# A third PSUM bank for a mixture-of-experts layer, and attention's turning and values in one bank

## The chip, the core and the metric

The kernel runs on one core of a Trainium2 chip. It uses the core's five engines: TensorE (matrix products), VectorE, ScalarE, GpSimd and SyncE, which issues nearly all the transfers. Each engine takes its own instructions in order and waits on semaphores for the others. The metric is the time on the device of one execution, in microseconds (us). Before the change it was 956.05 us, the median of three runs from 955.3 to 958.82.

## What is computed

Three layers follow each other: attention with a mask by blocks of 64 positions (8 batches, 8 heads, 576 positions, 64 dimensions a head), a dense layer with an exponential unit between two weight matrices (4608 tokens, 512 to 2048 and back to 512), and a soft mixture of 8 experts with 4 slots each.

```python
scores = scale * np.matmul(q, k.transpose(0, 1, 3, 2))
scores = np.where(block_i >= block_j, scores, -1e9)
attn = softmax(scores)                               # over the last axis
x = np.matmul(attn, v)                               # -> 4608 tokens x 512

h = x @ w_in                                         # 512 -> 2048, "first layer"
g = np.where(h > 0.0, h, np.exp(np.minimum(h, 0.0)) - 1.0)
x = g @ w_out                                        # 2048 -> 512

logits = x @ phi                                     # 512 -> 32 slots
d = softmax(logits, axis=0); slot_input = d.T @ x    # over all tokens
slot_out[e] = np.maximum(slot_input[e] @ w1[e], 0.0) @ w2[e]
c = softmax(logits, axis=1)
out = c @ slot_out
```

## The kernel before, in words

**Work units.** Attention is done for 32 pairs of heads (`n`, four pairs for each batch). The dense layer and the routing are done for 36 tiles of 128 tokens (`i`), and the first layer of a tile in four ranges of 512 columns (`r`). `w_out` is not applied to tokens: the product `w_out @ phi` is made at the start (`WP`), the logits come from the 2048 values `g` directly, and the slots gather `g`. The experts and the output follow in `tail`.

**Order.** Every step is entered into `Plan` with its engines, an estimated duration, the keys of what it reads and writes, and a due time (`key`). `Plan.order` simulates the engines with these estimates and each time gives a free engine the ready step with the smallest due time; the resulting order is the instruction order of the program. A tile has 22 units of due time, its ranges 5.5 each; a pair's steps start at a due time of its own and are spread over some 24 units. The planner knows of conflicts only what the keys say. What an instruction must really wait for is put in afterwards, from the memory that it touches.

**PSUM.** There are eight banks of 512 columns. `H0` and `H0 + 512` (keys `("h", 0)`, `("h", 1)`) take the first layer's ranges in turn, `GTB` the slot products, `POST` (key `"post"`) the routing, `SB0` and `SB0 + 512` the scores, `PTB` (key `"ptb"`) the turned weights of attention and the first 128 columns of the values, and `PVB` (key `"pvb"`) the other 448 columns of the values.

**A range** (`tile_range`, lines 800 to 828): 12 products into its bank (lines 808 to 810, in four steps of three), then ScalarE's exponent from the bank into a buffer `E` (line 813), VectorE's minimum and minus one on that buffer (line 815), and VectorE's maximum of the buffer and the bank into the range's output slot `g` (line 818). Only after the maximum is the bank free. For tiles 0 to 29 a stream transpose on VectorE (line 826) and two transfers (`tile_turn`) turn the output for the logits. There are 12 output slots for tiles 5 to 29, otherwise 8; four of the 12 lie in another area, which the trace calls att.

**Routing** (`tile_routing`, `tile_dispatch`): logits into `POST` columns 0 to 127 (line 853) and, in the same step, the slot products of the tile before into `GTB` (line 919); then copies, sums and maxima in `POST` up to column 415 (lines 876 to 904) in turn on VectorE, TensorE and ScalarE.

**A pair from the ninth on** (`n` at least 8): scores in four fills of the `SB0` banks (lines 564 to 577), row maxima (line 587), exponents (line 590), division on GpSimd (line 607), then some blocks turned by TensorE through `PTB` in three groups (`pair_swap`, line 700, through the transpose helper at line 360) and copied out on ScalarE or VectorE, and the others turned by stream transposes and transfers through DRAM (line 689, `swapped`). `swapped_values` then makes the products with the values (line 739): 18 of them, each in two passes, two running side by side on the two halves of the columns. The copy helper is at lines 336 and 338.

Of the kernel before, what the change touches and what calls it, by code (L numbers as in the profile page):

```python
# [18 lines left out]
P = 128  # L19
# [8 lines left out]
NEV, NQ = 16, 1  # L28
TLAG, LATE, NTP, JOINED = 2.5, 30, 8, 5
EARLY = 16.0  # L30
CHANGE, STAY, JOIN = 0.13, 0.0, 0.0
TICK, DUTY, FILL, FN = 3.4, 0.5, 0.055, 128
SCALE = 0.125
# [205 lines left out]
def attention_moe_kernel(ctx: ExitStack, tc, q, k, v, w_in, w_out, phi, w1, w2, consts, out):  # L239
# [13 lines left out]
    C = base.take(NTILE * NS)  # L253
# [57 lines left out]
    def f(o, n, p0=0, p1=P):  # L311
        return view(as_f32, o, n, p0, p1)
# [21 lines left out]
    def copy(e, o, i):  # L334
        if e == "ACT":
            nc.scalar.copy(o, i)  # L336
        else:
            nc.vector.tensor_copy(o, i)
# [10 lines left out]
    def evict(n, w):  # L349

        return (CP2, cpdur(w)) if n >= NEV else ("ACT", cpdur(w)[0])
# [317 lines left out]
    def swap_keys(sl):  # L669
        return [("px", sl, x) for x in UNITS] + [("px", sl, m) for m in range(len(MOVES))] + [("py", sl, g) for g in range(3)]  # L670
# [6 lines left out]
    def pair_swap(n, half, key):  # L677

        sl = n % 2
        px, py = PX + 4 * XW * sl, PY + 2 * YW * sl  # L680
        if n == NTP and half == 0:
            handover(swap_keys(0) + swap_keys(1), [x for y in range(NPT) for x in pt_keys[y]])
        for x in HALVES[half]:
            if x == "b" or x[0] == 0:
                continue
            cs = min(x[0] + 1, 3)
            at, _, step = spots(x[0], x[1], 0)
            o = f(px, 4 * XW).rearrange("p (m b j) -> p b m j", m=4, j=32)[:, at:at + step * (cs - 1) + 1:step]
            add("DVE", 0.12 + P * cs / 960, lambda e, x=x, o=o, cs=cs: nc.vector.transpose(  # L689
                out=o, in_=f(pat(x, n), P * cs).rearrange("p (c m i) -> p c m i", c=cs, m=4)),  # L690
                r=[pkey(x, n)], w=[("px", sl, x)], key=key)
        both = f(py, 2 * YW).rearrange("p (h w) -> p h w", h=2)
        groups = ([("b", c) for c in range(4)], [((3, 0), 3), ((3, 1), 3), ("b", 4)]) if half == 0 else ([((0, 0), 0), ((0, 1), 0)],)
        for gi, blocks in enumerate(groups):
            g = gi + 2 * half
            tb, tk = (PTB, "ptb")

            def tr(e, blocks=blocks, tb=tb):
                for j, (x, c) in enumerate(blocks):
                    transpose(pb(tb + P * j, P), f(pat(x, n) + P * c, P))  # L700
            add("PE", 0.02 + 0.108 * len(blocks), tr, r=[pkey(x, n) for x in {b[0]: 0 for b in blocks}] + ["con"], w=[tk], key=key, load=0.0)

            def evac(e, g=g, tb=tb):
                if g == 0:
                    src = pb(tb, 512).rearrange("p (c h x) -> p h c x", c=4, h=2)
                    copy(e, both[:, :, P:P + 192].rearrange("p h (c x) -> p h c x", c=3), src[:, :, 0:3])
                    copy(e, both[:, :, 448:512], src[:, :, 3])
                elif g == 1:
                    copy(e, both[:, :, 320:448], pb(tb, 256).rearrange("p (h x) -> p h x", h=2))
                    copy(e, both[:, :, 512:576], pb(tb + 256, P).rearrange("p (h x) -> p h x", h=2))  # L710
                else:
                    copy(e, both[:, :, 0:P], pb(tb, 256).rearrange("p (h x) -> p h x", h=2))
            add(*evict(n, (560, 430, 256)[g]), evac, r=[tk], w=[("py", sl, g)], key=key)
        if half == 0:
            return
        via = swapped[sl]
        load(via, f(px, 4 * XW), 4 * P * 4 * XW, r=[("px", sl, x) for x in UNITS], w=[("pvia", sl)], key=key, lag=TLAG)
        for j, (m, a0, a1) in enumerate(MOVES):
            load(f(px + XW * a0, XW * (a1 - a0), 32 * m, 32 * m + 32).rearrange("i (a y) -> i a y", y=XW),
                 via.rearrange("(a i) (m y) -> m i a y", a=4, m=4)[m][:, a0:a1], 200 * (a1 - a0) * XW,  # L720
                 r=[("pvia", sl)], w=[("px", sl, j)], key=key, lag=TLAG)

    def swapped_values(n, key):
        b, p = divmod(n, 4)
        sl = n % 2
        vs = V + 640 * (n % NV)
        px = f(PX + 4 * XW * sl, 4 * XW).rearrange("p (a b j) -> p b a j", a=4, j=32)
        both = f(PY + 2 * YW * sl, 2 * YW).rearrange("p (h w) -> p h w", h=2)
        ring = XR + RING * p + S * (b % 2)

        def far(h, c):
            u = max(c, 1)
            at, step, _ = spots(u, h, c)
            return px[:, at:at + step * (3 - u) + 1:step]

        def pv(e):
            def go(o, w, c, rhs, start, stop):
                for h in range(2):
                    mm(pb(o, w, 64 * h, 64 * h + 64), lhsT=f(vs + 320 * h + D * c, D), rhs=rhs(h), start=start, stop=stop)  # L739
            go(PTB, P, 0, lambda h: both[:, h, 0:P], True, True)  # L740
            for c in range(3):
                w = P * (4 - max(c, 1))
                go(PVB + 384 - w, w, c, lambda h: far(h, c), c == 0, False)
                go(PVB + 384, 64, c, lambda h: both[:, h, P + 64 * c:P + 64 * c + 64], False, False)
            go(PVB + 256, 192, 3, lambda h: both[:, h, 320:512], False, False)
            go(PVB + 384, 64, 4, lambda h: both[:, h, 512:576], False, True)
        add("PE", 3.0, pv, r=[("v", n % NV, j) for j in range(3)] + swap_keys(sl), w=["ptb", "pvb"], key=key, load=0.25, mode="C")
        add(*evict(n, P), lambda e: copy(e, f(ring, P), pb(PTB, P)), r=["ptb"], w=[("xr", p, b % 2, 0)], key=key)
        add(*evict(n, 448), lambda e: copy(e, f(ring + P, 448), pb(PVB, 448)), r=["pvb"], w=[("xr", p, b % 2, 1)], key=key)

    def pair_values(n, key):
        if n >= NTP:
# [45 lines left out]
            r=xr_keys + [("xh", s)], w=[("xl", s)], key=key)  # L798

    def tile_range(i, r, hb, gs, ts, kr):  # L800
        s = i % 2
        xh, xl = XH + 512 * s, XL + 512 * s
        g, gk = gs
        bank, ee = H0 + 512 * hb, E + 512 * hb
        for kk in range(4):
            def hm(e, kk=kk):
                hi, lo = fr(W[r] + 512 * kk, 512), fr(W[r] + PIECE + 512 * kk, 512)
                mm(pb(bank, 512), lhsT=fr(xh + P * kk, P), rhs=hi, start=(kk == 0), stop=False)  # L808
                mm(pb(bank, 512), lhsT=fr(xh + P * kk, P), rhs=lo, start=False, stop=False)  # L809
                mm(pb(bank, 512), lhsT=fr(xl + P * kk, P), rhs=hi, start=False, stop=(kk == 3))  # L810
            marks["hm"] = len(plan.ops)
            add("PE", 0.7, hm, r=[("xh", s), ("xl", s), ("wh", r, kk), ("wl", r, kk)], w=[("h", hb)], key=kr)
        add("ACT", 0.48, lambda e: nc.scalar.activation(f(ee, 512), pb(bank, 512), AF.Exp),  # L813
            r=[("h", hb)], w=[("e", hb)], key=kr)
        add("DVE", 0.335, lambda e: nc.vector.tensor_scalar(  # L815
            out=f(ee, 512), in0=f(ee, 512), scalar1=1.0, scalar2=-1.0, op0=ALU.min, op1=ALU.add),
            w=[("e", hb)], key=kr)
        add("DVE", 0.6, lambda e: nc.vector.tensor_tensor(  # L818
            out=f(g, 512), in0=f(ee, 512), in1=pb(bank, 512), op=ALU.max),
            r=[("e", hb), ("h", hb)], w=[gk], key=kr)  # L820

        if ts is None:

            hf = r // 2
            tt = f(TG[s] + 1024 * hf, 1024).rearrange("p (b c j) -> p c b j", b=4, j=32)[:, 4 * (r % 2):4 * (r % 2) + 4]
            add("DVE", 0.7, lambda e: nc.vector.transpose(out=tt, in_=f(g, 512).rearrange("p (c b i) -> p c b i", c=4, i=32)),  # L826
                r=[gk], w=[("tg", s, hf, "ab"[r % 2])], key=kr)
            return

        def gtr(e):  # L830
            for j in range(4):
                transpose(pb(GTB + P * j, P), f(g + P * j, P))
        add("PE", 0.44, gtr, r=[gk, "con"], w=["gtb"], key=kr, load=0.0)
        add(CP2, cpdur(512), lambda e: copy(e, f(ts[0], 512), pb(GTB, 512)), r=["gtb"], w=ts[1], key=kr)
# [133 lines left out]
    def tail(key):  # L968
# [61 lines left out]

        B = [512 * j for j in range(8)]
        bk = ["h0t", "h1t", "gtbt", "postt", "s0t", "s1t", "ptbt", "pvbt"]
        for nm, old in zip(bk, (("h", 0), ("h", 1), "gtb", "post", ("sb", 0), ("sb", 1), "ptb", "pvb")):
            handover([nm], [old])

# [199 lines left out]
```

## Time and profile before

| | |
|---|---|
| median of 3 runs | 956.05 us (955.3 to 958.82) |
| profiled execution | 955.77 us |
| span in its profile | 954.0 us |
| TensorE busy | 908.7 us, 95% |
| VectorE busy | 675.9 us, 71% |
| ScalarE busy | 439.4 us, 46% |
| GpSimd busy | 272.6 us, 29% |
| first product of tile 6, of tile 31 | 251.9, 782.7 us |
| mean granted clock of TensorE | 0.99 of full |

How to read it: the span runs from the first to the last instruction of one execution, and the runs' own time is a little longer. Busy time counts an engine's instructions at work, overlaps once; products are pipelined, so two that overlap count as one stretch, and a busy TensorE is not one at its peak. "Idle before" is the time in which nothing of an engine ran, put down to the instruction of another engine that came last before the next one started. In the rows PE is TensorE, DVE VectorE, ACT ScalarE, and L808 is line 808.

### The profile page before, as it was taken

Reading aid. Unit: us, or ns where it says so; the run is one execution under the profiler, and the core shown is the slowest. Engines: PE = TensorE matmul, PEld = TensorE weight load, DVE = VectorE, ACT = ScalarE, POOL = GpSimd, SP = SyncE. Lnnn points to the kernel's source line nnn. Section 1 sums busy time; section 2 is a strip of 40 time slices with the busy share of each in tenths; the row PEclk is TensorE's granted clock in tenths of the full one; section 3 lists DMA queues with packets and bytes.
Section 4 is the critical chain, followed back from the end, with each engine's and each line's share of the span. In section 5 each row is a group of like instructions: output and inputs, shape, how many; then the busy total and the mean of one; then the engine's idle time right before and its main releaser. Section 6 shows DMA issues by size and latency. Waiting matters only on the chain.

```text
span 954.0 us, 19403 instructions
## 1 busy us (share of the span) xinstructions
PE 908.7 (95%) x6708; PEld 623.3 (65%) x6708; DVE 675.9 (71%) x1718; ACT 439.4 (46%) x1285; POOL 272.6 (29%) x428
## 2 busy tenths in 40 slices
PE   8889999999999999999999999999999999999992
PEld 6556777666666766676766666766776776766350
DVE  5887795668787887777888878887887844333160
ACT  5775655445445535444445445444444333322143
POOL 2863442133342332222323432332332210000000
PEclk9999999999999999999999999999999999999996
DMA  9846755647777785767677777667756498068969
GB/s 235 243 130 171 220 184 159 146 115 207 202 203 218 197 209 184 212 181 211 194 203 206 199 208 201 202 188 203 206 163 217 144 305 340 3 216 298 377 223 342
DMA packets 253217, 197.08 MB, mean 207 GB/s; under 512 B 183232, under 2 KB 206400, under 8 KB 250048
## 3 DMA queue, kind: packets, MB, share of 16 engines
q1 hardware_dynamic: 251920, 195.55, 69.1%
q8 instruction: 54, 0.88, 0.4%
q10 hardware_dynamic: 1200, 0.30, 0.1%
q14 instruction: 43, 0.35, 0.1%
HBM read 125.52 MB, written 70.25 MB: 205 GB/s over the span
## 4 chain that ended last, share of the span: by engine, by line
PE 74%; DVE 8%; DMA 7%; SPq 4%; ACT 2%; issue 2%; POOL 1%; ACTq 0%; DVEq 0%; POOLq 0%
PE ps L808 13%; PE ps L810 11%; PE ps L809 11%; PE ps L360 8%; PE ps L576 7%; PE ps L739 7%; SPq L355 4%; PE ps L919 3%; PE ps L568 2%; PE ps L853 2%; DMA att<-swapped 2%; DMA swapped<-att 2%; PE ps L767 2%; DVE base L587 2%; PE ps L460 1%
## 5 line engine op out<-in xcount | busy, mean ns | idle before, releaser
L808 PE MATMUL ps<-w,xhl 128*128 128x512 f32 x576 | 249.8, 434 | 7.8 <-DVE g L818 5.5
L607 POOL TENSOR_SCALAR att<-att,base 128x128 f32<-128x128 f32 (+4 forms) x288 | 181.0, 647 | 222.2 <-DVE base L603 151.0
L810 PE MATMUL ps<-w,xhl 128*128 128x512 f32 x576 | 226.8, 394 | 0.0
L809 PE MATMUL ps<-w,xhl 128*128 128x512 f32 x576 | 225.7, 392 | 0.0
L590 ACT ACTIVATE att<-ps,base 128x128 f32<-128x128 f32 (+4 forms) x288 | 157.4, 552 | 122.9 <-DVE base L587 121.0
L587 DVE TENSOR_REDUCE base<-ps 128x1 f32<-128x128 f32 (+4 forms) x288 | 135.7, 503 | 21.3 <-PE ps L572 12.2
L808 PEld LDWEIGHTS ps<-w,xhl 128*128 128x128 f32 x576 | 108.8, 189 | 52.0 <-issue 19.1
L813 ACT ACTIVATE xe<-ps 128x512 f32<-128x512 f32 x144 | 86.0, 600 | 115.0 <-PE ps L810 113.7
L810 PEld LDWEIGHTS ps<-w,xhl 128*128 128x128 f32 x576 | 108.1, 188 | 24.9
L336 ACT COPY att<-ps 128x128 f32<-128x128 f32 (+3 forms) x192 | 75.7, 434 | 95.8 <-PE ps L360 90.6
L809 PEld LDWEIGHTS ps<-w,xhl 128*128 128x128 f32 x576 | 108.9, 189 | 14.8
L815 DVE TENSOR_SCALAR xe<-xe 128x512 f32<-128x512 f32 x144 | 68.1, 473 | 67.0 <-ACT xe L813 65.6
L576 PE MATMUL ps<-att 64*128 64x128 f32 (+3 forms) x512 | 96.1, 468 | 1.0 <-ACT att L590 1.0
L360 PE MATMUL ps<-base,att 128*128 128x128 f32 (+1 forms) x496 | 83.2, 282 | 9.7 <-POOL att L607 8.5
L360 PEld LDWEIGHTS ps<-base,att 128*128 128x128 f32 (+1 forms) x496 | 58.0, 143 | 44.5 <-POOL att L607 17.6
L795 POOL TENSOR_TENSOR xhl<-xe,xhl 128x512 fp32r<-128x512 f32 x36 | 46.3, 1291 | 133.1 <-ACT xhl L793 127.0
L818 DVE TENSOR_TENSOR g<-xe,ps 128x512 f32<-128x512 f32 x108 | 73.3, 680 | 2.4
L689 DVE STREAM_TRANSPOSE att<-att 128x384 f32<-128x384 f32 x144 | 70.4, 507 | 5.3 <-POOL att L607 4.2
L739 PE MATMUL ps<-att 128*64 128x64 f32 (+4 forms) x864 | 71.9, 318 | 1.2 <-DMA att<-swapped 0.7
L576 PEld LDWEIGHTS ps<-att 64*128 64x128 f32 x512 | 42.0, 185 | 40.6 <-issue 14.1
L739 PEld LDWEIGHTS ps<-att 128*64 128x64 f32 x864 | 46.8, 137 | 32.3 <-issue 23.6
L826 DVE STREAM_TRANSPOSE g<-g 128x512 f32<-128x512 f32 x84 | 58.0, 695 | 1.7 <-DMA turned<-g 0.2
(134 smaller groups left out, 1115.1 us busy)
## 6 DMA issues: line engine op xcount, KB each, us to landing
turned<-g SPq DMA_DIRECT2D x60, 512.0 KB, 3.1
swapped<-att SPq DMA_DIRECT2D x24, 1024.0 KB, 4.6
g<-turned SPq DMA_DIRECT2D x120, 96.0 KB, 2.6
att<-in_moe_w_dram SPq DMA_DIRECT2D x11, 1024.0 KB, 11.8
att<-swapped SPq DMA_DIRECT2D x48, 192.0 KB, 3.9
att<-in_v_dram SPq DMA_DIRECT2D x64, 128.0 KB, 3.2
g<-in_moe_w_in_dram SPq DMA_DIRECT2D x16, 512.0 KB, 5.3
w_late<-in_moe_w_dram SPq DMA_DIRECT2D x8, 1024.0 KB, 6.9
```

The lines of the kernel that those rows point to most:

```text
L336: nc.scalar.copy(o, i)
L360: mm(o, lhsT=i, rhs=f(IDN + base, n, base, base + n), start=True, stop=True, is_transpose=True)
L576: mm(pb(at((u, h)), P * (u + 1)), lhsT=f(qt + P * u, P, 64 * h, 64 * h + 64), rhs=f(kt, P * (u + 1), 64 * h, 64 * h + 64), start=True, sto ...
L587: add("DVE", 0.08 + wide(x) / 960, lambda e, x=x, c=c: nc.vector.tensor_reduce(out=f(c, 1), in_=pb(at(x), wide(x)), axis=AX.X, op=ALU.max, ...
L590: add("ACT", 0.50 + wide(x) / 1300, lambda e, x=x, c=c: nc.scalar.activation(f(pat(x, n), wide(x)), pb(at(x), wide(x)), AF.Exp, bias=f(c, ...
L607: add("POOL", (0.28 + wide(x) / 1050) * (1.3 if n < 8 else 1.0), lambda e, x=x, p=p: nc.gpsimd.tensor_scalar(out=f(p, wide(x)), in0=f(p, w ...
L739: mm(pb(o, w, 64 * h, 64 * h + 64), lhsT=f(vs + 320 * h + D * c, D), rhs=rhs(h), start=start, stop=stop)
L808: mm(pb(bank, 512), lhsT=fr(xh + P * kk, P), rhs=hi, start=(kk == 0), stop=False)
L809: mm(pb(bank, 512), lhsT=fr(xh + P * kk, P), rhs=lo, start=False, stop=False)
L810: mm(pb(bank, 512), lhsT=fr(xl + P * kk, P), rhs=hi, start=False, stop=(kk == 3))
L813: add("ACT", 0.48, lambda e: nc.scalar.activation(f(ee, 512), pb(bank, 512), AF.Exp), r=[("h", hb)], w=[("e", hb)], key=kr)
L818: add("DVE", 0.6, lambda e: nc.vector.tensor_tensor(out=f(g, 512), in0=f(ee, 512), in1=pb(bank, 512), op=ALU.max), r=[("e", hb), ("h", hb) ...
```

## The change

From tile 6 to tile 33 the ranges of the first layer take three banks in turn, the third being `PTB`. In these tiles the exponent is written to the output slot and minimum and maximum work there in place; the buffer `E` isn't used. For pairs from the ninth on, the turned groups and the first 512 columns of the values go through `PVB`, and the last 64 columns of the values into the last 64 columns of `POST` under a new key `"pvx"`. The products of the values are split anew (20 instead of 18, the same columns in all), and the two copies are of 512 and 64 columns instead of 128 and 448.

```diff
+THREE = (6, 34)
 ...
@@ pair_swap
-            tb, tk = (PTB, "ptb")
+            tb, tk = (PVB, "pvb")
@@ swapped_values
-            go(PTB, P, 0, lambda h: both[:, h, 0:P], True, True)
+            go(PVB, P, 0, lambda h: both[:, h, 0:P], True, True)
             for c in range(3):
                 w = P * (4 - max(c, 1))
-                go(PVB + 384 - w, w, c, lambda h: far(h, c), c == 0, False)
-                go(PVB + 384, 64, c, lambda h: both[:, h, P + 64 * c:P + 64 * c + 64], False, False)
-            go(PVB + 256, 192, 3, lambda h: both[:, h, 320:512], False, False)
-            go(PVB + 384, 64, 4, lambda h: both[:, h, 512:576], False, True)
-        add("PE", 3.0, pv, r=[("v", n % NV, j) for j in range(3)] + swap_keys(sl), w=["ptb", "pvb"], key=key, load=0.25, mode="C")
-        add(*evict(n, P), lambda e: copy(e, f(ring, P), pb(PTB, P)), r=["ptb"], w=[("xr", p, b % 2, 0)], key=key)
-        add(*evict(n, 448), lambda e: copy(e, f(ring + P, 448), pb(PVB, 448)), r=["pvb"], w=[("xr", p, b % 2, 1)], key=key)
+                go(PVB + 512 - w, w, c, lambda h: far(h, c), c == 0, False)
+            go(PVB + 384, P, 3, lambda h: both[:, h, 320:448], False, True)
+            for c in range(5):
+                x = P + 64 * c if c < 3 else 64 * c + 256
+                go(POST + 448, 64, c, lambda h: both[:, h, x:x + 64], c == 0, c == 4)
+        add("PE", 3.0, pv, r=[("v", n % NV, j) for j in range(3)] + swap_keys(sl), w=["pvb", "pvx"], key=key, load=0.25, mode="C")
+        add(*evict(n, 512), lambda e: copy(e, f(ring, 512), pb(PVB, 512)), r=["pvb"], w=[("xr", p, b % 2, 0)], key=key)
+        add(*evict(n, 64), lambda e: copy(e, f(ring + 512, 64), pb(POST + 448, 64)), r=["pvx"], w=[("xr", p, b % 2, 1)], key=key)
@@ tile_range
+        three = THREE[0] <= i < THREE[1]
+        if three:
+            hb = (4 * i + r) % 3
+        if (i, r) == (THREE[0], 0):
+            handover([("h", 2)], ["ptb"])
-        bank, ee = H0 + 512 * hb, E + 512 * hb
+        bank, ee, ek = ((H0, H0 + 512, PTB)[hb], g, gk) if three else (H0 + 512 * hb, E + 512 * hb, ("e", hb))
 ...
         add("ACT", 0.48, lambda e: nc.scalar.activation(f(ee, 512), pb(bank, 512), AF.Exp),
-            r=[("h", hb)], w=[("e", hb)], key=kr)
+            r=[("h", hb)], w=[ek], key=kr)
 ...
-            w=[("e", hb)], key=kr)
+            w=[ek], key=kr)
 ...
-            r=[("e", hb), ("h", hb)], w=[gk], key=kr)
+            r=[ek, ("h", hb)], w=[gk], key=kr)
@@ tail
+        handover(["ptb"], [("h", 2)])
+        handover(["post"], ["pvx"])
```

## Rows read from the trace of the kernel before

**Rows 1.** The page, part 1: busy us (share of span) and instructions of each engine.

```profile
PE 908.7 (95%) x6708; PEld 623.3 (65%) x6708; DVE 675.9 (71%) x1718; ACT 439.4 (46%) x1285; POOL 272.6 (29%) x428
```

**Rows 2.** Busy us by stretch: PE, PEld, DVE, ACT, POOL (instructions), clock, DMA share, GB/s.

```profile
251.90:782.70 530.80, 522.58 (x3772) 364.46 (x3770) 426.23 (x1124) 241.57 (x765) 164.87 (x281) 1.00 0.71 201
...
866.50:954.00 87.50, 66.18 (x574) 32.79 (x574) 26.17 (x52) 26.50 (x55) 0.00 (x0) 0.91 0.86 313
```

**Rows 3.** Waits of TensorE from 250 to 782.7: us in total, times, longest.

```profile
PE ps L808 <- DVE g L818: 3.5, 5, 0.9
PE ps L808 <- DVE att L818: 2.2, 3, 1.0
PE ps L360 <- DVE base L924: 0.9, 1, 0.9
...
PE ps L360 <- ACT base L889: 0.2, 1, 0.2
```

**Rows 4.** Waits of TensorE from 120 to 250.

```profile
PE ps L808 <- DVE g L818: 2.0, 1, 2.0
```

**Rows 5.** Instructions in order, 343.5 to 348: start, us, engine, line, [idle before <-releaser].

```profile
345.42 0.40 PE L810 MATMUL ps<-w,xhl 128*128 128x512 f32 x1
...
346.00 0.69 DVE L818 TENSOR_TENSOR g<-xe,ps 128x512 f32<-128x512 f32 x1
...
346.75 0.50 PE L808 MATMUL ps<-w,xhl 128*128 128x512 f32 x1 [0.93 <-DVE g L818]
...
346.99 0.60 ACT L813 ACTIVATE xe<-ps 128x512 f32<-128x512 f32 x1
347.08 0.40 PE L809 MATMUL ps<-w,xhl 128*128 128x512 f32 x1
347.31 0.39 PE L810 MATMUL ps<-w,xhl 128*128 128x512 f32 x1
```

**Rows 6.** Instructions in order, 334.5 to 344: values, logits and slot products, an exponent.

```profile
335.69 2.95 PE L739 MATMUL ps<-att 128*64 128x128 f32 x36
...
338.57 1.08 PE L853 MATMUL ps<-g,base 128*32 128x128 f32 x32
...
339.46 1.04 PE L919 MATMUL ps<-g,base 128*32 128x512 f32 x8
...
342.52 0.60 ACT L813 ACTIVATE xe<-ps 128x512 f32<-128x512 f32 x1 [2.88 <-PE ps L810]
```

**Rows 7.** Instructions in order, 473.5 to 479: values, their second copy, turning.

```profile
473.92 2.95 PE L739 MATMUL ps<-att 128*64 128x128 f32 x36
...
477.05 0.58 DVE L338 COPY xe<-ps 128x448 f32<-128x448 f32 x1
...
477.44 0.66 PE L360 MATMUL ps<-base,att 128*128 128x128 f32 x4
```

**Rows 8.** Line 336, ScalarE's copies of the values: ns min/median/max, first and last start, forms.

```profile
L336 ACT COPY xe<-ps x51: 202/267/598, 42.7 to 776.0; 128x128 f32<-128x128 f32 x23, 128x448 f32<-128x448 f32 x12, 128x64 f32<-128x64 f32 x8, 128x512 f32<-128x512 f32 x8
```

**Rows 9.** Instructions in order, 659 to 664.5: routing steps during the values.

```profile
660.04 2.95 PE L739 MATMUL ps<-att 128*64 128x128 f32 x36
...
660.68 0.25 DVE L885 TENSOR_REDUCE base<-ps 128x1 f32<-128x128 f32 x1
...
661.41 0.36 ACT L889 ACTIVATE base<-ps,base 128x128 f32<-128x128 f32 x1
...
662.92 0.33 PE L360 MATMUL ps<-base 128*128 128x128 f32 x1
```

**Rows 10.** TensorE in order, 764 to 786: last pair's values, tile 31.

```profile
776.34 2.73 PE L739 MATMUL ps<-att 128*64 128x384 f32 x32 [0.49 <-DMA att<-swapped]
...
781.81 0.66 PE L360 MATMUL ps<-base,g 128*128 128x128 f32 x4 [0.87 <-DVE base L924]
...
782.67 0.48 PE L808 MATMUL ps<-w,xhl 128*128 128x512 f32 x1
```

## The prediction

> **What bounds the kernel now.** I read the busy times first [rows 1]. TensorE is busy for 908.7 of 954.0 us, VectorE for 71% of it and the others for less. The profiled execution took 955.77 us by the clock of the runs, 1.8 more than its span; the median of the three runs shown is 956.05. All sums below are made against the profiled execution, and 0.3 is added at the end to come to the median.
>
> The stretches by stage come next [rows 2]. From the start of tile 6 to the start of tile 31 (251.9 to 782.7 us) TensorE is busy 522.6 of 530.8 us, at the full one of its two clock levels (granted clock 1.00, 2.4 GHz). It is therefore the bound there, and only 8.2 us of idle time is left. In the tail, from 866.5 us on, it is busy 66 of 87.5 us; the change does nothing there but come to it earlier or later.
>
> The waits say whose fault the idle time is [rows 3]. In that stretch 5.7 of the 8.2 us is the first product of a range (line 808) waiting for the maximum of an older range on VectorE (line 818): five waits of 3.5 us where the values go into a slot of the one area, three of 2.2 us where they go into one of the spare slots. That is the wait for a free first-layer bank: a product may not overwrite a bank before the maximum has read it. One more of 2.0 us lies ahead of tile 6 [rows 4], where the change leaves two banks, so it is not counted.
>
> One such wait in full [rows 5]: the last product of a range starts at 345.42, the first of the next at 346.75. Products inside a range start 0.23 us apart (347.08, 347.31). So TensorE lost 1.33 - 0.23 = 1.10 us, where the idle column says 0.93, since a product still runs for 0.17 us after the next could have started. In that time VectorE made the maximum of the range two before (346.00 to 346.69); ScalarE began the exponent of the range just finished only at 346.99.
>
> **The change, part by part.**
>
> **A third bank** (tiles 6 to 33). The first product of a range now waits for the maximum three ranges back. Removed: 5.7 us of idle [rows 3] plus 8 waits of 0.17 us that the idle column hides [rows 5], 7.1 us in all. Does the older maximum come in time? VectorE ends one maximum per range, and a range is 12 products, at least 12 x 0.23 = 2.8 us, so the maximum before it is normally older than the longest wait, 1.0 us [rows 3]. I take all 7.1 us. What is next late at such a place: the products run on, and ScalarE and VectorE work off the same queue, so TensorE comes to the next bank 1.1 us earlier and finds the one just released. Bounds: nothing (the lateness of VectorE moves to the next step that needs it) and 8.2 us (all idle time of the stretch).
>
> **Exponent in place.** No instruction is added or taken away; exponent, minimum and maximum go on the same shapes, so they cost the same. ScalarE now waits for the output slot itself, which the products over the slots (line 919) of three tiles before must have read. At the tightest place that I found those products start at 339.46 and run 1.04 us, and the first exponent of the tile that takes the slot starts at 342.52 [rows 6]: 2.0 us in hand. Taken as nothing; without that cover it would cost up to 2.8 us (one range earlier) at a few tiles.
>
> **Turning and values in one bank.** Before, the values used two banks and the turning shared one of them, so values and turning already took turns; what is new is that turning after the values waits for the copy of 512 columns and not of 128. Where turning follows at once [rows 7], the products of the values start at 473.92 and run 2.95 us, to 476.87, the copy of 448 columns is done at 477.63, and the turning starts at 477.44, so a hop past such a copy is 0.2 to 0.4 us later than now. About two thirds of the 24 pairs have turning within 1.1 us of the values. The order is planned with this wait, and TensorE has range products to put there. Bounds: 0 and 16 x 0.35 = 5.6 us; I take 0.3 us, since in the list of waits of the stretch turning (line 360) appears only with the routing's own steps (lines 924 and 889) and never with a copy [rows 3].
>
> **Products and copies of the values.** The products of a pair stream the same 1,600 columns in 20 instead of 18 (each in two passes: 36 instructions in 2.95 us now [rows 7]). By columns that is 0; by instructions 4 x 0.08 = 0.32 us a pair, 7.7 us for 24. I take 0, because the added ones are narrow and two run side by side, and keep the other end for the upper side. The copies are 512 + 64 columns instead of 128 + 448, the same sum; a short copy costs 0.2 us [rows 8].
>
> **The 64 columns in the routing's bank.** The last 64 columns of the values go into bank POST, columns 448 to 511, under a key of their own, while the routing (lines 850 to 910) uses columns 0 to 415 under key "post". So the planner lays both out as if they never met. Nothing in the trace of before shows two such uses of one bank at a time. If they need no turns, this costs 0. If every use of the bank has to wait for the one issued before it on another engine, two things happen. First: at 7 of the 24 pairs the logits come directly behind the values, as at 338.57, 2.88 us after their start [rows 6]; the copy of the 64 columns, ready 0.2 us later, is then issued behind them and waits until they and the slot products in the same step have run (338.57 to 339.46 + 1.04 = 340.50), 1.9 us in which ScalarE or VectorE stands with all that is queued behind. Second: at 3 pairs a reading of the bank falls into the values, as at 660.68 and (ScalarE) 661.41 [rows 9], and would wait for their end at 662.92, some 2.5 us; behind it on VectorE wait minima and maxima of the ranges and the row maxima of attention, and for these ScalarE and TensorE. Together 7 x 1.9 + 3 x 2.5 = 20.8 us of standing engines; that is the other end. What reaches TensorE: where a late VectorE cost it anything, it cost 7.1 us in 8 waits, 0.9 each [rows 3, 5]. The third bank covers range products, not scores and turning, so I let half of the 10 cases through: 5 x 0.9 = 4.4 us.
>
> The Trainium skill ("PSUM — Partial Sum Buffer", section "PSUM bank collisions raise a hardware error") states that TensorE, VectorE and ScalarE may not be at one bank and quadrant at once, at disjoint columns either, and tells to guard by bank. That speaks for turns and against this part of the change; no run here shows it yet.
>
> **Sum:** 955.8 - 7.1 + 0.3 + 4.4 = 953.4 in the profiled execution's terms, some 953.5 by the median.
>
> **The rivals.**
>
> **Shared bank for nothing.** The routing and the 64 columns meet without harm, or engines that stand have slack: 955.8 - 7.1 + 0.3 + 0 = 949.0. For it: ScalarE is busy 46% of the span [rows 1]. Against: VectorE is busy 426 of 530.8 us in the stretch [rows 2] and is the engine that is late already.
>
> **The waits move.** The third bank does not do what it says, because VectorE still owes the same work and the next product that needs it (scores, turning, routing) takes over the wait, or because the last pair becomes the bound: its values wait for a transfer at 776.34 and end at 779.0, TensorE then waits 0.87 us, and tile 31 starts at 782.67 [rows 10], so each us by which the last pair is late is lost there. Everything between 954 and 958; 956.
>
> **Turns at the routing's bank decide.** Slower than before: the 20.8 us of standing engines reach TensorE by more than a third (7.1 of 20.8), at the places named. By six tenths it is 955.8 - 6.8 + 12.5 = 961.5, in full 970. For it: the planner does not know of it and can't put other work there, and TensorE takes its instructions in order. Against: the values last 2.9 us, in which TensorE needs nobody, and a range more is free to run.
>
> **How the numbers follow.** Forecast 953.5 (its own range 951 to 956): 0.40. Shared bank for nothing, 949 (946.5 to 951): 0.25. The waits move, 956: 0.19. Turns decide, 961.5 to 970: 0.16. About 0.5%, 4.8 us, is what a measurement of this kernel can tell from no change, so faster means below 951.3 and slower above 960.8. Faster: 0.25 and 0.05 of the forecast's lower edge, 0.30. Slower: 0.16. Within: 0.54. The range goes from 947 to 962; it leaves out the edge below and the upper part of the last rival, some 0.15, and takes in the first part of the price by instructions.
>
> **What would show it right or wrong.** Line 808 should lose its waits for line 818 between tiles 6 and 31 (5.7 us to under 1). If they stay, the third bank is not the point. New waits of the 64-column copy (line 750 or so of the new kernel, through the copy helper) for the logits or slot products, and of the routing's VectorE steps for the values' products, would show the turns; their count times 1.9 and 2.5 us is the bound above. Turning (line 360) that waits for copies of the values would show the price of the single bank. The prediction is wrong if TensorE's busy time in the stretch itself moves by several us (other changes between kinds of products in the new order), for which I have no price.

## The result, and the profile after

The changed kernel takes 966.41 us (median of four runs, 962.30 to 970.11) where the kernel before, on the same chip, takes 955.67 (the three runs of the table and a fourth): a ratio of 1.0102, 95% interval 1.0057 to 1.0147, so slower by 1.0%. The forecast was 953.5 with a range from 947 to 962. The result lies where the third rival put it ("turns at the routing's bank decide", 961.5 to 970). One execution of 3046.84 us, of a kernel further down (the 64 columns in `GTB`), is left out of its median and ratio.

The profiled execution of after took 968.14 us, with a span of 966.3; before it was 955.77 and 954.0. First the busy times and the clock line of the page of after (the last digit of that line is the tail, as before).

```profile
PE 914.8 (95%) x6804; PEld 629.9 (65%) x6804; DVE 666.9 (69%) x1712; ACT 446.2 (46%) x1291; POOL 273.2 (28%) x428
...
PEclk9999999999999999899999999999999999999996
```

TensorE is busy 6.1 us more than in [rows 1], and one slice in the middle shows a lower clock. Where the time lies is told by the stretches of after: us, then busy us (instructions) of PE, PEld, DVE, ACT and POOL, clock, DMA share, GB/s. The first is from the start of tile 6 to the start of tile 31, as in [rows 2].

```profile
251.40:796.20 544.80, 529.04 (x3890) 371.31 (x3888) 423.04 (x1128) 248.38 (x774) 163.47 (x282) 0.99 0.70 198
404.20:411.00 6.80, 5.43 (x17) 4.02 (x17) 4.45 (x10) 1.66 (x8) 3.11 (x5) 0.50 0.90 238
455.40:458.80 3.40, 3.40 (x11) 2.68 (x10) 2.34 (x6) 1.90 (x6) 2.75 (x6) 0.50 0.67 147
708.00:711.40 3.40, 3.40 (x10) 1.97 (x7) 1.43 (x4) 1.44 (x4) 0.94 (x1) 0.50 0.90 342
```

The stretch is 14.0 us longer than before (544.8 against 530.8). Idle time is 15.8 us where it was 8.2, so 7.5 us more; busy time is 6.5 us more. Nearly all of the busy part is the clock. Three times TensorE is at the lower level (granted clock 0.50, that is 1.2 GHz): 404.2 to 411.0, 455.4 to 458.8 and 708.0 to 711.4. It works for 12.2 us of these 13.6 us, and half of that, some 6.1 us, is lost. In before the level is full throughout the stretch [rows 2]. The start (0.5 us) and what follows tile 31 (1.2 us) are shorter than before, which leaves 12.3 us of span.

What TensorE waits for in that stretch: us in all, times, longest.

```profile
PE ps L361 <- ACT base L896: 6.2, 4, 3.4
PE ps L740 <- DMA att<-swapped: 1.8, 2, 1.0
PE ps L361 <- ACT att L337: 1.8, 2, 1.1
PE ps L887 <- DVE base L883: 1.1, 3, 0.5
PE ps L569 <- ACT att L591: 1.1, 1, 1.1
...
PE ps L361 <- ACT base L903: 0.5, 1, 0.5
```

Lines are moved by 1 to 7: 808 is now 815, 818 is 825, 739 is 740, 360 is 361, 876 is 883, 880 and 881 are 887 and 888, 885 is 892, 889 is 896, 896 is 903. No wait of line 815 for line 825 is left here: the 5.7 us of [rows 3] are gone, as foretold. At the head stands a kind of wait that was 0.2 us in [rows 3]: the product that turns the routing's weights (the flip, line 361) waits for ScalarE's exponents (lines 896 and 903). Why they are late is told by the waits of VectorE and ScalarE for the products of the values (line 740):

```profile
DVE base L892 <- PE ps L740: 4.8, 1, 4.8
DVE base L883 <- PE ps L740: 2.1, 1, 2.1
...
ACT base L903 <- PE ps L740: 5.2, 2, 2.8
```

In before nothing but the copies of the values waits for those products. Now three steps of the routing do: the copy of the logits, the row maximum, an exponent. They read columns 0 to 287 of `POST`; the values write columns 448 to 511 of it. One place in full (instructions in order: start, us, engine, line, with the idle time before it in brackets):

```profile
396.66 2.96 PE L740 MATMUL ps<-att 128*64 128x128 f32 x40
...
399.67 0.29 DVE L883 COPY base<-ps 128x128 f32<-128x128 f32 x1 [2.12 <-PE ps L740]
...
400.34 0.31 PE L888 MATMUL ps<-base 128*128 128x32 f32 x2
...
403.61 0.25 DVE L892 TENSOR_REDUCE base<-ps 128x1 f32<-128x128 f32 x1
...
405.05 0.37 ACT L896 ACTIVATE base<-ps,base 128x128 f32<-128x128 f32 x1 [0.68 <-DVE base L894]
...
405.57 0.47 PE L361 MATMUL ps<-base 128*128 128x128 f32 x1 [3.43 <-ACT base L896]
405.69 0.77 PE L815 MATMUL ps<-w,xhl 128*128 128x512 f32 x1
...
406.26 0.63 PE L816 MATMUL ps<-w,xhl 128*128 128x512 f32 x1
...
412.34 0.39 PE L816 MATMUL ps<-w,xhl 128*128 128x512 f32 x1
```

VectorE stands for 2.12 us until the last of the 40 matmuls of the values has ended at 399.62. The chain copy, sums, maximum, exponent, flip starts that much later, with VectorE's other work in between, and TensorE, which takes its instructions in order, comes to the flip and stands for 3.43 us. Behind it a first-layer product takes 0.63 us, where it takes 0.39 six microseconds later. The four other places, by their steps:

```profile
376.77 0.29 ACT L903 ACTIVATE base<-ps,base 128x32 f32<-128x32 f32 x1 [2.82 <-PE ps L740]
...
452.63 0.37 ACT L896 ACTIVATE base<-ps,base 128x128 f32<-128x128 f32 x1 [2.82 <-issue]
...
701.84 0.29 ACT L903 ACTIVATE base<-ps,base 128x32 f32<-128x32 f32 x1 [2.35 <-PE ps L740]
...
792.19 0.29 DVE L892 TENSOR_REDUCE base<-ps 128x1 f32<-128x128 f32 x1 [4.82 <-PE ps L740]
```

At 452.63 the trace names no releaser, but the step starts 0.10 us after the end of the values that began at 449.47. Together the engines stand for 2.12 + 2.82 + 2.82 + 2.35 + 4.82 = 14.9 us at 5 of the 24 pairs. At each of the five the flip then keeps TensorE waiting: 6.2 us in four waits and 0.5 us in one. Three of the five places lie ahead of the three stretches at the lower clock, the last of them by 6 us.

### The profile page after: what moved, and what is told of

Same layout as the page of the kernel before. It is cut to its first block, busy times and chain, and to the rows that moved or that the text cites. A ratio compares the mean times of both kernels' runs of the same rounds, so it can differ in the third digit from the quotient of the medians.

```text
span 966.3 us, 19599 instructions
## 1 busy us (share of the span) xinstructions
PE 914.8 (95%) x6804; PEld 629.9 (65%) x6804; DVE 666.9 (69%) x1712; ACT 446.2 (46%) x1291; POOL 273.2 (28%) x428
## 4 chain that ended last, share of the span: by engine, by line
PE 81%; DVE 6%; DMA 5%; ACT 2%; issue 2%; POOL 2%; SPq 1%; ACTq 0%; DVEq 0%; POOLq 0%
PE ps L815 14%; PE ps L817 13%; PE ps L816 13%; PE ps L361 8%; PE ps L577 8%; PE ps L740 7%; PE ps L926 3%; PE ps L860 3%; PE ps L569 2%; PE ps L461 1%; POOL att L608 1%; PE ps L769 1%; DMA att<-in_moe_w_dram 1%; PE ps L1110 1%; SPq L356 1%
## 5 line engine op out<-in xcount | busy, mean ns | idle before, releaser
L740 PE MATMUL ps<-att 128*64 128x128 f32 (+2 forms) x960 | 71.8, 303 | 2.4 <-DMA att<-swapped 1.8
L820 ACT ACTIVATE g<-ps 128x512 f32<-128x512 f32 x80 | 47.7, 598 | 50.0 <-PE ps L817 48.7
L822 DVE TENSOR_SCALAR g<-g 128x512 f32<-128x512 f32 x80 | 36.8, 461 | 39.1 <-ACT g L820 38.3
L591 ACT ACTIVATION_READ_ACCUMULATOR att<-ps,base 128x1 f32 x288 | 57.8, 201 | 0.0
```

The costliest lines, as they stand in the source:

```text
L591: add("ACT", 0.50 + wide(x) / 1300, lambda e, x=x, c=c: nc.scalar.activation(f(pat(x, n), wide(x)), pb(at(x), wide(x)), AF.Exp, bias=f(c, ...
```

## The experiments

My theory after the result was that the 64 columns in `POST` make turns, and that these and the clock behind them are the loss. The rivals: the plan's new order costs the time; the one bank for turning and values costs it; the third bank brings new waits.

**The same order without the turns.** The 64 columns go to `PVB`, as the products' only bank, and the short copy reads a constant of the same shape, so the last 64 columns of each pair's result are left out. Every engine keeps its order of instructions.

```diff
-                go(POST + 448, 64, c, ...)
+                go(PVB + 448, 64, c, ...)
-        add(*evict(n, 64), lambda e: copy(e, f(ring + 512, 64), pb(POST + 448, 64)), ...)
+        add(*evict(n, 64), lambda e: copy(e, f(ring + 512, 64), f(IDN, 64)), ...)
```

> The changed kernel with its order of instructions unchanged, but the last 64 columns of the values go into the last 64 columns of PVB instead of POST, and the 64-column copy reads constants from SBUF instead of that bank (so the last 64 columns of each pair's values are wrong and computed in vain). TURNS (the 64 columns and the routing must take turns at bank POST, and the planned order does not know it): the copy of the logits on VectorE no longer waits for the end of the values, the 3.4 us wait of the routing's flip near 405 us and the half clock behind it are gone, and the time falls from 966 to 948 to 953 us, below the kernel before. ORDER (the new plan itself is worse, or the third bank moves the waits elsewhere): the time stays at 962 to 970 us with the same long waits.

Measured: 954.6 us beside 955.46, ratio 0.9989 (0.9964 to 1.0013). Order and amount of work are those of after, so the turns are what made it slow; the rivals of order and of the single bank can't carry it. But the 7 us of the third bank are not there either. Its stretch from tile 6 to tile 31, one piece of it at half clock, the waits of TensorE, and the place of the longest:

```profile
251.20:783.00 531.80, 523.62 (x3869) 368.82 (x3867) 422.26 (x1127) 246.18 (x772) 162.60 (x280) 0.99 0.70 200
397.00:403.70 6.70, 5.62 (x38) 3.71 (x39) 2.49 (x5) 0.41 (x1) 2.58 (x6) 0.52 0.35 117
...
PE ps L740 <- DMA att<-swapped: 3.0, 1, 3.0
PE ps L361 <- ACT att L337: 1.5, 2, 0.8
PE ps L740 <- DMA g<-turned: 1.4, 2, 1.1
...
394.68 0.44 PE L740 MATMUL ps<-att 128*64 128x128 f32 x4
...
398.08 5.17 PE L740 MATMUL ps<-att 128*64 128x384 f32 x36 [2.96 <-DMA att<-swapped]
```

The stretch has 8.2 us of idle time, as much as before, though 5.7 us of it had gone. The last pair of the third batch waits for its transfers (3.0 us; in before such a wait is 0.49 us [rows 10]), and the 36 matmuls behind it take 5.17 us at clock 0.52, where such products of another last pair in before, 32 matmuls in the row, take 2.73 at full clock [rows 10].

**Which half of the turns.** Two kernels, each with one edit of the pair above: in one only the products go to `POST`, in the other only the short copy reads from there (what it reads is then not the values).

> The changed kernel in its own order; the last products of the values still go to POST, but the 64-column copy reads constants from SBUF instead of that bank (the last 64 columns of the values are computed and not used). What is left of the turns: a routing step on VectorE or ScalarE that is issued behind the values waits for their end. PRODUCTS (these waits are the cost, as seen at 399.7 and 701.8 us): 963 to 969 us, ratio 1.007 to 1.013. COPY (the copy that waits for the routing is the cost): 953 to 957 us, ratio 0.997 to 1.001.

> The changed kernel in its own order; the last products of the values go to the last 64 columns of PVB (so those columns are wrong there), but the 64-column copy still reads the last 64 columns of POST, which nobody writes in this stretch. What is left of the turns: the copy waits for routing steps issued before it, and routing steps issued behind it wait for the copy. PRODUCTS: 953 to 957 us, ratio 0.997 to 1.001. COPY: 960 to 966 us, ratio 1.005 to 1.012.

Measured, beside 957.04: products to `POST` 967.19 (ratio 1.0116, 1.0090 to 1.0142), copies from `POST` 954.95 (0.9989, 0.9967 to 1.0012). The first is after again, the second the kernel without turns. The waits of VectorE and ScalarE for the values in the first:

```profile
DVE base L892 <- PE ps L740: 3.9, 1, 3.9
DVE base L883 <- PE ps L740: 2.1, 1, 2.1
...
ACT base L903 <- PE ps L740: 5.2, 2, 2.8
```

In the second there is no such row for a routing step; its short copies do wait for the logits, seven times, and that costs nothing that can be told. So all of the price, 12.2 us between the two, lies with routing steps that wait for the end of the values' products. How much of it are the waits? The flip, in the first kernel and then in the second (two rows each, the longest wait last), and the short copies of the second:

```profile
PE ps L361 <- ACT base L896: 6.2, 4, 3.4
...
406.17 0.48 PE L361 MATMUL ps<-base 128*128 128x128 f32 x1 [3.43 <-ACT base L896]
...
PE ps L361 <- ACT base L896: 1.2, 1, 1.2
...
402.07 0.33 PE L361 MATMUL ps<-base 128*128 128x128 f32 x1 [1.19 <-ACT base L896]
...
DVE xe L339 <- PE ps L860: 6.5, 4, 2.8
...
ACT xe L337 <- PE ps L860: 1.3, 3, 0.4
```

With the 0.5 us behind line 903 the five flips wait 6.7 us with the turns. Without them four do not wait, and the one of the longest wait still waits 1.2 us. So 5.5 us of idle time are the turns'. The mean granted clock of the executions was 0.9835 and 0.988; by 960 us that is an estimate of 4.3 us for the clock. Some 2 us of the 12.2 have no row of their own.

**The turns alone, in the order of before.** In the kernel before, the last 64 columns of the values (one group of products instead of the last of five that add up) go to `POST`, and the second copy becomes one of 384 and one of 64 columns; the sum over the last 64 columns is left out except for one term.

```diff
-            go(PVB + 256, 192, 3, lambda h: both[:, h, 320:512], False, False)
-            go(PVB + 384, 64, 4, lambda h: both[:, h, 512:576], False, True)
+            go(PVB + 256, 192, 3, lambda h: both[:, h, 320:512], False, True)
+            go(POST + 448, 64, 4, lambda h: both[:, h, 512:576], True, True)
```

> The kernel before with its own order of steps, two first-layer banks and two banks for attention; only the last of the products with the values (64 columns) goes to POST columns 448 to 511 instead of PVB, and the second copy takes 384 columns from PVB and 64 from POST (the last 64 columns of each pair's values thereby lack four of their five terms). TURNS: the unplanned turns at POST alone cost 4 to 12 us on the old order, 960 to 968 us, with VectorE's routing steps waiting for the values. ORDER: 955 to 958 us, no more than one added short copy for each of 24 pairs (24 x 0.2 us on ScalarE or VectorE, mostly beside other work).

Measured: 957.75, ratio 1.0031 (1.0011 to 1.0052). Here three steps are caught:

```profile
DVE base L908 <- PE ps L739: 6.2, 2, 3.3
...
DVE base L889 <- PE ps L739: 2.3, 1, 2.3
```

VectorE stands for 8.5 us, more than half of the 14.9 in after, yet only 2.3 us (by the interval 1.1 to 5.0) reach the end. Line 908 copies the flipped weights; the slot products that read them come a tile later, and no wait of TensorE for line 908 is in the trace. What turns cost goes with the steps that they catch, in these two kernels.

**The exponent in place, alone.** In the kernel before, with two banks:

```diff
-        bank, ee = H0 + 512 * hb, E + 512 * hb
+        bank, ee, ek = (H0 + 512 * hb, g, gk) if three else (H0 + 512 * hb, E + 512 * hb, ("e", hb))
```

> The kernel before with only the exponent in place in tiles 6 to 33; two first-layer banks, attention's banks as before. Both theories: same time, 954 to 957 us, unless the wait for the output slot shifts the planned order; a change above 959 us would put the blame on the exponent in place.

Measured: 954.58, ratio 0.9996 (0.9980 to 1.0011). It costs nothing.

**All but the third bank, with the turns and without.** `THREE = (99, 99)` in after, and the same in the kernel without turns.

> The changed kernel without its third bank and without the exponent in place (two banks for the first layer in all tiles, PTB idle from the ninth pair on); attention in one bank and the last 64 columns in POST as in the change. TURNS: 958 to 968 us with the first-layer waits of 5 to 7 us and VectorE or ScalarE waiting for the values. If the third bank itself does the harm: 955 to 957 us.

> The kernel two_banks (no third bank, attention in one bank) with its order unchanged, but POST left untouched in the way of same_order (the last 64 columns of each pair's values are wrong). TURNS: the 4.8 us by which two_banks is slower than the kernel before are the turns at POST: 954 to 957 us. SHARED BANK (turning and values in the one bank PVB cost it): it stays at 959 to 962 us.

Measured: 960.28, ratio 1.0067 (1.0043 to 1.0091), and 962.25 beside 957.75, ratio 1.0053 (1.0028 to 1.0077). TensorE and VectorE in the first:

```profile
PE ps L815 <- DVE g L825: 6.6, 8, 1.2
PE ps L740 <- DMA att<-swapped: 2.1, 1, 2.1
PE ps L815 <- DVE att L825: 2.1, 3, 0.9
...
DVE base L911 <- PE ps L740: 6.3, 2, 3.3
```

The first-layer waits are back (8.7 us, where before has 5.7). The turns are there too, but both catch line 911, the copy of the flipped weights, and cost little: the two ratios agree. So what frees the bank (turning and values in one, the products split anew, and the order that the planner makes of it) costs some 0.5%, about 5 us. The third bank then gives 0.64% (1.0053 to 0.9989, both without turns), some 6 us, and the turns in after's order take 1.2%. These kernels each have an order of their own, so the two shares are no cleaner than that.

**Telling the planner.** In after, the values write the key `"post"` instead of `"pvx"`; in a second kernel the 64 columns go to `GTB` under its key `"gtb"`; in a third they are made by a second step of TensorE in `PVB`, after the copy of 512 columns.

```diff
-  w=["pvb", "pvx"], key=key, load=0.25, mode="C")
+  w=["pvb", "post"], key=key, load=0.25, mode="C")
```

> The changed kernel, but the planner is told: the products with the values write the key post instead of pvx, and the 64-column copy reads it. Everything computed is as in the changed kernel. TURNS: the planner lays values and routing one behind the other; no VectorE routing step waits for the values, but the order is tighter: 949 to 957 us. ORDER: 960 us or more, since the third bank and the shared bank PVB stay.

> The changed kernel with the last 64 columns of the values in the slot bank GTB instead of POST, under that bank's key, so that the planner knows of the turns. The slot bank is held for some 3 us a tile, the routing bank for 5 to 6. If turns that are planned cost little: 950 to 957 us. If, as with the key post (970 us), every planned turn on a busy bank holds the values or the routing back: 960 to 970 us.

> The changed kernel, but the last 64 columns of the values are a second step in PVB after the copy of the first 512 columns, so POST is left alone and the planner knows of everything. TURNS: 949 to 955 us: the third bank's 7 us less one more use of PVB and up to two more changes of the kind of products for each pair (24 x 0.1 to 0.3 us). ORDER: 960 us or more.

Measured: 970.11 (1.0142, 1.0113 to 1.0171), 960.14 (1.0060, 1.0043 to 1.0076) and 961.82 (1.0057, 1.0032 to 1.0081). Knowing of the bank, the planner may not start the values until the routing is through with it, and in the first kernel the wait lands on the flip all the same:

```profile
PE ps L361 <- ACT base L896: 6.6, 5, 2.1
PE ps L887 <- DVE base L883: 2.6, 2, 1.4
...
511.96 0.48 PE L361 MATMUL ps<-base 128*128 128x128 f32 x1 [2.06 <-ACT base L896]
```

The values, which could have filled that time, follow only at 512.36. In the third kernel the waits are no longer than in before, but TensorE is busy for longer. From tile 6 to the last first-layer product, before and then the third kernel:

```profile
251.85:866.20 614.35, 605.91 (x4336) 423.16 (x4334) 460.09 (x1202) 268.40 (x828) 168.74 (x284) 1.00 0.69 201
...
252.90:871.70 618.80, 612.33 (x4428) 422.58 (x4427) 456.10 (x1191) 274.89 (x839) 169.12 (x284) 1.00 0.68 200
```

Idle are 6.5 us instead of 8.4, busy 6.4 us more. Counted in the trace, TensorE changes the shape of its products (rows and columns of the array in use) 276 times there instead of 232. If all of the 6.4 us are theirs, which is not shown, a change costs some 0.14 us; the 0.1 to 0.3 us of the expectation had no row behind them.

**Where the 7 us went: transfers.** The kernel without turns, whose six transfers of turned weights land in spare columns that no product reads, in 8 of the 12 slices (what the values take from them is not the turned weights). The orders stay the same.

> The kernel same_order (the changed kernel's order, POST untouched) with one difference: the transfers that bring the swapped blocks of a pair back into SBUF land in spare columns that the values do not read, and bring 8 of 12 slices (the values therefore use the blocks as they were, and are wrong). No product waits for these transfers any more; orders of all engines are the same. BOUNDARY (what the third bank saved was lost again where the last pair of a batch waits for its transfers, 3.0 us at tile 13, and in the half clock behind that wait, 6.8 us at half level or 3.4 us lost): 947 to 950 us, the half level near 400 us gone. SPREAD (the gain went in many small waits on VectorE and ScalarE): 953 to 955 us.

Measured: 952.1, ratio 0.9968 (0.9949 to 0.9987). The wait of 3.0 us and the slow stretch behind it are gone, and the flip behind them waits 1.7 us where it waited 0.7. This lies between the two expectations: by the ratios it gives back 0.2%, about 2 us of the 7, and the two intervals overlap, so that even this is not clear of noise.

**Where the 7 us went: the plan.** Starting the pairs of a batch 4 units of due time earlier (`EARLY` 20 for 16) should bring the transfers earlier. Done in the kernel before, in the one without turns, and in the one with the 64 columns in `GTB`.

> The kernel before with one number changed: attention from the ninth pair on is due up to 4 units earlier (EARLY 20 instead of 16). A control for what a newly planned order does by itself, with no bank changed. If the order is not sensitive: 954 to 957 us. If small shifts of the order alone move the time by several us, other newly planned kernels differ from the kernel before by as much without cause: 950 to 965 us.

> The kernel same_order (third bank, POST untouched, last 64 columns of the values wrong) with attention due up to 4 units earlier, so newly planned. BOUNDARY (range products run ahead with the third bank and then wait for the last pair of a batch): the last pair comes in time, no wait for swapped transfers above 1 us, 947 to 951 us. SPREAD: 953 to 957 us.

> The kernel told_gtb (third bank, the last 64 columns in the slot bank with its key; computes everything) with attention due up to 4 units earlier. BOUNDARY: 951 to 956 us, at or below the kernel before. SPREAD or planned turns: 958 to 962 us as before.

Measured, beside 957.75: 961.49 (1.0043, 1.0016 to 1.0070), 962.96 (1.0051, 1.0023 to 1.0078) and 959.08 (1.0019, 0.9996 to 1.0041). The second was to be 947 to 951, or 953 to 957 by the other theory, and missed both. Its waits of TensorE:

```profile
PE ps L577 <- ACT att L591: 3.1, 2, 2.9
...
PE ps L740 <- DMA att<-swapped: 0.3, 1, 0.3
```

So the wait for the transfers is cured, from 3.0 to 0.3 us, and others stand in its place: the 7 us do not lie in that wait alone. The first kernel says how far a new order alone can carry, in this one case: 0.4%, more than half of the gain that was sought. The third is the best complete kernel with a third bank, and no better than before.

## Why the prediction was wrong

**The third bank: right.** The waits of line 808 went from 5.7 us to none, and with everything else of the change in place it is worth some 6 us where the sum took 7.1.

**Exponent in place: right,** nothing, as [rows 6] said.

**Turning and values in one bank: too small.** The sum took 0.3 us, with 5.6 as the other end (the trace of before has turning within 1.1 us of the values at 13 pairs, not 16, which makes 4.6); the kernels with everything but the third bank measure some 5 us. It does not come the way the bound was made, by turning that waits for copies of the values: in after that is one wait of 0.3 us. With two banks it shows as a wait for transfers (one of 2.1 us) and as longer waits for first-layer banks (8.7 us for 5.7), in an order that is new throughout; no single row carries it. Together with the third bank this makes the second rival, "the waits move", at 956: without turns at `POST` the stretch has 8.2 us of idle time as before, in other places, and the kernel ends within 0.4% of before. Turning that waits for copies of turned weights (line 361 for line 337) is one such place: 1.5 us there, and none in [rows 3].

**Products by columns: right.** 20 products run 2.96 us, 18 ran 2.95 [rows 7].

**The 64 columns in the routing's bank: the failed step.** The sum took 4.4 us, from 10 cases of which half come through at 0.9 us. Three things were wrong in it.
- The seven copies at 1.9 us each are two thirds of the bound of 20.8 us. Copies do wait for the logits seven times, 7.8 us in all with the copies' turns alone, and the kernel is no slower for it. The copies of 64 columns have slack, and what is queued behind them too.
- The readings were counted in the order of before: three at 2.5 us. In that order the count was right: three steps stand for 8.5 us, and 2.3 us reach the end, less than the sum took. But the change makes a new order, and in it there are five, which stand for 14.9 us; the values catch the chain of logits, sums, maximum, exponent and flip in its middle. The 0.9 us that a late VectorE cost was taken from waits on a range's maximum [rows 3], where work of other ranges is queued. On this chain TensorE's own next instruction is the end of the chain, and every one of the five came through, with 5.5 us in all.
- The clock was in no term. In after half clock follows three of the five places and makes the work there 6.1 us longer; over the executions of the kernels with and without the turns the estimate is 4.3 us.

In its own order the term measures 12.2 us, between the kernels that differ in it alone. It lies near the 12.5 us that the rival took for six tenths of the bound, but by another way than the rival worked it out: that the two numbers meet is luck. In after steps on columns 0 to 287 waited 2.1 to 4.8 us for products into columns 448 to 511; line 883 is one of them, and in the kernel without turns it does not wait. The Trainium skill ("PSUM — Partial Sum Buffer", section "PSUM bank collisions raise a hardware error") states that disjoint columns of a bank are no excuse. The waits follow that rule, but it is the program that puts them in; what the chip would do if the two met without a wait, no run here shows.

**What stays open.** Whether the 5 us for freeing the bank are the single bank's or the new order's: a new order alone moves 4 us. One wait for transfers was taken away and gave back about 2 us, hardly clear of noise; the others were not tried one by one.

## What to carry to other kernels

When a planner orders the work by keys, one physical bank needs one key: two keys in a bank make turns that no order takes account of, but before giving it the one key, look whether the bank is one through which a chain of short steps runs, since then the planned wait costs as much. To price such a turn, don't count the standing engines; ask whether the step that is caught is the one whose result TensorE needs as its next instruction. And when a buffer is taken from one use and given to another, price the use that loses it as carefully as the one that gains: here they were worth 5 and 6 us.

## What the hardware showed

**Half clock after a wait.** TensorE's granted clock fell to half (1.2 GHz) in or behind single idle times of 2.96 us (the kernel without turns, half from 397.3 to 404.1) and 3.43 us (after), in the middle of a stretch where it had been full. The products then started 0.43 us apart instead of 0.23 and took 0.63 instead of 0.39 us. In after 5.4 us of work fell into the piece behind the wait of 3.43 us, so the wait cost itself and some 2.7 us more. What follows a wait is not the same each time: with the products' turns alone the same wait of 3.43 us was followed by half clock from 405.7 to 409.1 only, and the other four flips by none. The wait of 2.0 us ahead of tile 6 [rows 4] was followed by the full level in before and after, and by the half level (clock 0.56 from 212.6 to 216) in the kernel without turns, whose instructions up to there are those of after. And in after half clock came at 708.0 where no single wait was long: TensorE waited 0.48, 1.06 and 0.72 us within five microseconds.

**Executions of one kernel differ in it.** The four of after had 962.3, 964.7, 968.1 and 970.1 us at mean clocks of 0.988, 0.987, 0.981 and 0.983: the two quicker ones at the higher clock, though not in strict order.
